# Attention with two score banks: the banks made one tile for joined converts on VectorE, GpSimd instructions in halves, a freer limit for zero-weight passes

## Chip, cores, metric

One core of one Trainium2 chip. The metric is the device time of one execution in microseconds, the median of repeated runs. PE is TensorE, DVE VectorE, ACT ScalarE, POOL GpSimd.

## What must be computed

Two attention blocks over the same input of 2048 rows and 512 columns (32 heads of 16), mixed by a gate per row:

```python
def reference(A_x, A_wqkv, A_wo, B_x, B_wqkv, B_wo, gate_w):
    x = A_x
    g = sigmoid((x * gate_w).sum(-1, keepdims=True))
    a = full_attention(x, A_wqkv, A_wo)          # softmax(q k^T / 4) v, 32 heads, S = 2048
    b = local_dilated_attention(x, B_wqkv, B_wo) # each row sees 8 rows, 2 apart
    return g * a + (1 - g) * b
```

Block A is the bulk: 32 heads x 2048 x 2048 scores, each of which needs an exponential.

## The kernel before

A planner, written in Python, runs while the kernel is built. It places every instruction on its engine by a table of durations and emits them in that order; on the chip each engine follows its fixed order, and semaphores make it wait where data is not there yet. (In the trace of before the 1012 instructions of VectorE, 669 of ScalarE and 589 of GpSimd all start in the order of the built program, compared by what they write and read, and so do 10810 of TensorE's 10822 matmuls; the other 12 have changed places, in pairs, with the one beside them. ScalarE waits 27.5 us for the rings there, in 36 waits.) So the plan's durations never bind the chip (half a multiplication of GpSimd, planned at 600 ns, takes 669 in halves_alone), but its **order** does.

Scores go two ways. Most tiles (128 x 512) are filled by TensorE into one of two "rings" of PSUM banks, and ScalarE takes their exponential. The rest, in quads of four tiles, are filled into one of two single banks, and VectorE "converts" them: one multiply-add with a 16-bit integer result, whose bits read as bfloat16 approximate the exponential, then two additions of a constant for a better fit. The two banks also take every projection of the kernel. GpSimd does the elementwise work of block B. Zero-weight matmul passes ("zero passes") are there to keep TensorE at its full clock: without them the time at half clock (a granted clock of 0.5) grows.

```python
# before: each bank is a buffer of its own (tag m0 or m1), taken anew for each use
def misc_ps(hold, shape, dtype=FP32):
    return ps.tile(shape, dtype, tag=f"m{hold.k}", bufs=1, name=f"m{hold.k}_ps")
# ... one tile of a quad (cut)
def fill(j=j, hold=hold, st=st):
    st["s"] = misc_ps(hold, [128, QW])
    for _ in range(f_.zeros):
        mm_ct(st["s"], zw, ones_t[:], True, True)
    mm(st["s"][:], kt_all[32*j:32*j+32, i, t*128:(t+1)*128], qt_tiles[...], True, True, tile_position=(32*j, 0))
def conv(j=j, st=st):
    V.tensor_scalar(out=q["terms"][0][:, j, :], in0=st["s"][:], scalar1=EXP_MULT, scalar2=EXP_ADD, ...)
# ... GpSimd, block B (cut)
G.tensor_tensor(out=st["prod"][:, w_ % 2, :], in0=st["ksh"][:, w_, :], in1=st["qb"][:], op=ALU.mult)   # planned at 1149 ns
# ... limit for a zero pass (cut)
if sh >= high or after > (first + 60.0 if sh >= low else alone + 230.0):
    return
```

## Time and profile before

| | before |
|---|---|
| time | 806.65 us (3 runs, 806.61 to 809.28) |
| busy | ScalarE 93%, TensorE 91%, VectorE 80%, GpSimd 70% |
| half clock of TensorE, first to last exponential | 41 us in 6 stretches |
| ScalarE idle, first to last exponential | 28 us |
| chain of waits | ScalarE 50%, TensorE 27%, VectorE 11% |

TensorE's share is no measure of its load, as its matmuls overlap: the 1620 fills of the rings, 388 ns each or 629 us one after another, keep it busy for 277.8 us. ScalarE's share is a better one, as its instructions overlap by only 0.2 us each. The last row follows the execution back from its end, at each step to what released the instruction: half of the span is exponentials that followed one another. This is its line on the page of before ("issue" is time for which the profile shows no cause; SPq, ACTq and DVEq are the instruction queues of SyncE, ScalarE and VectorE):

```profile
ACT 50%; PE 27%; DVE 11%; issue 9%; SPq 2%; DMA 1%; ACTq 0%; DVEq 0%
```

Engines, clock and waits of before are shown in the prediction below.

### The profile page before, as it was taken

The numbers are of one execution on the slowest core, as the hardware profiler recorded it, in microseconds if no ns is written. First come the engines' busy times: TensorE is split into PE (matmuls) and PEld (weight loads), VectorE is DVE, ScalarE is ACT, GpSimd is POOL, SyncE is SP. The second block draws the span as 40 slices with busy tenths as digits, with TensorE's granted clock in tenths as the row PEclk, the third lists the DMA queues.
The fourth block names the chain that finished last, engine by engine and source line by source line (L and its number), as shares of the span: only waits on it lengthen the run. The fifth ranks groups of instructions, "written<-read, shape, count | busy, mean of one in ns | idle before, by whom it ended". The sixth has DMA issues, their size and how long they took to land.

```text
span 806.9 us, 24993 instructions
## 1 busy us (share of the span) xinstructions
PE 736.5 (91%) x10822; PEld 245.6 (30%) x10822; DVE 649.1 (80%) x1012; ACT 747.0 (93%) x670; POOL 561.1 (70%) x589
## 2 busy tenths in 40 slices
PE   7898999998898999999989999988999899999996
PEld 3242232323232223333233223323233223322332
DVE  5757997788977767889978999997879997777765
ACT  2998898999999979999999999999899999999991
POOL 1017888598519957697969698979788898995500
PEclk9999998999999879999999999999899999999998
DMA  9332031422302221414211404031313130402000
GB/s 205 106 112 86 30 104 48 139 87 72 105 3 98 81 77 49 140 35 138 81 47 35 137 5 132 19 102 58 108 53 112 34 105 25 142 24 84 9 15 34
DMA packets 66798, 62.07 MB, mean 77 GB/s; under 512 B 14848, under 2 KB 64128, under 8 KB 66688
## 3 DMA queue, kind: packets, MB, share of 16 engines
q1 hardware_dynamic: 65104, 60.28, 24.0%
q8 instruction: 84, 1.38, 0.7%
q10 hardware_dynamic: 1584, 0.20, 0.2%
q14 instruction: 26, 0.21, 0.1%
HBM read 43.91 MB, written 12.62 MB: 70 GB/s over the span
## 4 chain that ended last, share of the span: by engine, by line
ACT 50%; PE 27%; DVE 11%; issue 9%; SPq 2%; DMA 1%; ACTq 0%; DVEq 0%
ACT pT L390 49%; PE m_ps L390 11%; PE acc L390 9%; DVE dt L390 8%; PE ring L390 7%; SPq L390 2%; DVE qr L390 1%; ACT lg L390 1%; DMA xT<-in_A_x_dram 0%; DVE accT L390 0%; DVE kvs L390 0%; DVE osb L390 0%; DVE kmax_all L390 0%; DVE vd_all L390 0%; DMA kt_all<-kr 0%
## 5 line engine op out<-in xcount | busy, mean ns | idle before, releaser
L390 ACT ACTIVATE pT<-ring 128x1536 bf16<-128x1536 f32 (+1 forms) x648 | 741.9, 1335 | 28.7 <-PE ring L390 27.5
L390 DVE TENSOR_SCALAR dt<-m_ps 128x512 uint16<-128x512 f32 x428 | 283.7, 680 | 74.1 <-PE m_ps L390 57.2
L390 PE MATMUL ring<-qt,kt_all 32*128 32x512 bf16 x1620 | 277.8, 388 | 39.7 <-ACT pT L390 34.9
L390 DVE TENSOR_SCALAR dt<-dt 128x2048 uint16<-128x2048 uint16 x214 | 203.6, 964 | 3.0 <-PE acc L390 1.9
L390 PEld LDWEIGHTS <-kt_all 32*128 32x128 bf16 (+1 forms) x2304 | 95.0, 91 | 312.9 <-issue 299.5
L390 POOL TENSOR_TENSOR prod<-prod 128x512 f32<-128x512 f32 (+2 forms) x192 | 175.4, 914 | 8.8
L390 POOL TENSOR_TENSOR prod<-ksh,qb 128x512 f32<-128x512 bf16 x128 | 158.5, 1257 | 11.4 <-DMA ksh<-kv_scr 8.8
L390 POOL TENSOR_TENSOR pv<-vsh,lg 128x512 bf16<-128x512 bf16 x128 | 152.5, 1198 | 15.4 <-PE m_ps L390 13.9
L390 PE MATMUL m_ps<-qt,kt_all 32*128 32x512 bf16 x428 | 148.7, 386 | 10.4 <-DVE dt L390 7.3
L390 PE MATMUL acc<-pT,vp_all 128*17 128x512 bf16 x1620 | 133.4, 390 | 0.0
L390 POOL TENSOR_TENSOR ott<-accT,rden 128x256 bf16<-128x256 f32 x31 | 24.1, 777 | 89.6 <-DVE rden L390 89.5
L390 PE MATMUL acc<-dt,vd_all 128*17 128x512 bf16 x856 | 76.3, 385 | 0.0
L390 PE MATMUL acc<-ones_t,zw 128*32 128x512 bf16 x744 | 66.4, 393 | 0.0
L390 PE MATMUL m_ps<-bw,xT 128*32 128x512 bf16 x768 | 59.4, 406 | 3.6 <-DVE kvs L390 2.0
L390 PEld LDWEIGHTS <-vp_all 128*17 128x17 bf16 x2048 | 41.9, 89 | 68.4 <-issue 55.1
L390 PEld LDWEIGHTS <-xT 128*32 128x32 bf16 (+1 forms) x1920 | 34.5, 98 | 36.9 <-issue 28.6
L390 PE MATMUL acc<-dt,vp_all 128*17 128x512 bf16 x428 | 42.5, 388 | 0.0
L390 POOL TENSOR_TENSOR lg<-lg,mx 128x256 f32<-128x256 f32 x16 | 12.0, 748 | 41.8 <-DVE mx L390 41.8
L390 PE MATMUL m_ps<-ident,pv 128*32 128x128 bf16 x2048 | 39.3, 220 | 0.2 <-DVE dt L390 0.2
L390 POOL TENSOR_TENSOR lg<-lg,rr 128x256 f32<-128x256 f32 x16 | 10.7, 670 | 40.2 <-DVE rr L390 34.2
L390 DVE CAST kvs<-m_ps 128x512 bf16<-128x512 f32 x32 | 21.8, 683 | 17.4 <-PE m_ps L390 17.1
L390 PEld LDWEIGHTS <-pv 128*32 128x32 bf16 x2048 | 30.4, 96 | 14.8 <-issue 11.8
(82 smaller groups left out, 412.8 us busy)
## 6 DMA issues: line engine op xcount, KB each, us to landing
ksh<-kv_scr SPq DMA_DIRECT2D x16, 1024.0 KB
vsh<-kv_scr SPq DMA_DIRECT2D x16, 1024.0 KB
kv_scr<-kvs SPq DMA_DIRECT2D x16, 384.0 KB
q_scr<-qr SPq DMA_DIRECT2D x32, 128.0 KB
qt<-q_scr SPq DMA_DIRECT2D x31, 128.0 KB
qb<-kv_scr SPq DMA_DIRECT2D x16, 128.0 KB
out_dram<-osb SPq DMA_DIRECT2D x16, 128.0 KB
kt_all<-kr SPq DMA_DIRECT2D x112, 16.0 KB
```

The lines of the kernel that those rows point to most:

```text
L390: return chain_on(key, f(*a, **k))
```

## The change

Its intent: relieve VectorE by converting two tiles in one instruction where both banks are free; let VectorE's additions be held up less by GpSimd, by halving GpSimd's long instructions; and admit more zero passes where the activity that the planner counts is low. How GpSimd holds them up is seen in the trace of before: 141 of the 214 additions of 128x2048 see a GpSimd instruction end while they run, and they themselves end 545 to 683 ns after it, 550 at the median. To convert two banks in one instruction, the change makes them one tile: `mm_t` replaces the two buffers. (The diff is shortened; `...` marks a cut. A count that goes with the halves, from 25 to 37 instructions of GpSimd, is left out.)

```diff
-    def misc_ps(hold, shape, dtype=FP32):
-        return ps.tile(shape, dtype, tag=f"m{hold.k}", bufs=1, name=f"m{hold.k}_ps")
+    mm_t = ps.tile([128, 2, QW], FP32, tag="mm", bufs=1, name="mm_ps")
+    def misc_ps(hold, shape):
+        v = mm_t[:, hold.k, 0:math.prod(shape[1:])]
+        ...
-            if sh >= high or after > (first + 60.0 if sh >= low else alone + 230.0):
+            if sh >= high or after > (first + 60.0 if sh >= low else alone + 450.0):
-            padd(lmul(w_), 1149.0, ...)                    # and amul 1094, ltree 1260
+            padd(lmul(w_, 0), 600.0, ...)                  # two halves; amul 575, ltree 630
+        def conv(j):
+            V.tensor_scalar(out=q["terms"][0][:, j:j + 2, :] if j in both else q["terms"][0][:, j, :],
+                            in0=mm_t[:] if j in both else mm_t[:, holds[j].k, :], ...)
+        def join(j, at):     # called when fill j (0 or 2) is placed
+            if S_.slots["m"].when(2) + (MARGIN["DVE", "PE"] if at > 25000.0 else 0.0) > at + JOIN:   # JOIN = 100
+                return
+            both.add(j)      # one fill of two matmuls, one convert of 1217 ns
```

More of the change, by code (lines that the diff above doesn't have):

```diff
@@ L78 @@
                  "name", "not_before", "after", "begun", "prompt", "zeros", "closing",
-                 "lock", "gap", "kb")
+                 "lock", "gap", "kb", "ahead")
     def __init__(self, eng, fn, dur=0.0, mms=None, deps=(), due=None, allow=1000.0, acq=(), rel=(), lat=0.0,
@@ L83, in __init__ @@
                  lock=False, kb=0.0):
+        self.ahead = None
         self.kb = kb
@@ L207, in commit @@
         e = op.eng
+        if op.ahead is not None:
+            op.ahead(max(ready, self.t[e]))
         for h in op.acq:
@@ L418 @@
         S_.slots["keep"].free[k] = INF
-    def misc_ps(hold, shape, dtype=FP32):
-        return ps.tile(shape, dtype, tag=f"m{hold.k}", bufs=1, name=f"m{hold.k}_ps")
+    mm_t = ps.tile([128, 2, QW], FP32, tag="mm", bufs=1, name="mm_ps")
+    def misc_ps(hold, shape):
+        v = mm_t[:, hold.k, 0:math.prod(shape[1:])]
+        if len(shape) > 2:
+            v = v.rearrange("p (a b) -> p a b", a=shape[1])
+        return v
     def sb(hold, shape, dtype, name):
@@ L897, in padd @@
         def padd(fn, dur, after_last=True, early=False, **kw):
-            late = len(pool) > 25 and not early
+            late = len(pool) > 37 and not early
             o = Op("POOL", fn, dur=dur, due=float(2 * t + (3 if late else 0)), name="bp", **kw)
@@ L903, in padd, with lmul @@
             return o
-        def lmul(w_):
+        HD = D // 2
+        def lmul(w_, lo):
             def s():
-                if w_ % 2 == 0:
+                if w_ % 2 == 0 and lo == 0:
                     st["prod"] = work.tile([128, 2, D], FP32, name="prod", tag="prod", bufs=1)
@@ L910, in s, with ltree @@
                         st["lg"] = sb(hlg, [128, H, W], FP32, "lg")
-                G.tensor_tensor(out=st["prod"][:, w_ % 2, :], in0=st["ksh"][:, w_, :], in1=st["qb"][:], op=ALU.mult)
+                G.tensor_tensor(out=st["prod"][:, w_ % 2, lo:lo + HD], in0=st["ksh"][:, w_, lo:lo + HD], in1=st["qb"][:, lo:lo + HD],
+                                op=ALU.mult)
             return s
-        def ltree(w_, n):
+        def ltree(w_, n, a=0, b=2):
             def s():
-                pv_ = st["prod"][:].rearrange("p w (h d) -> p w h d", d=DH)
+                pv_ = st["prod"][:, a:b, :].rearrange("p w (h d) -> p w h d", d=DH)
                 if n > 1:
@@ L923, in b_tile @@
         for w_ in range(0, W, 2):
-            padd(lmul(w_), 1149.0, after_last=w_ > 0, acq=[hlg] if w_ == 0 else [], deps=[lk] if w_ == 0 else [])
-            padd(lmul(w_ + 1), 1149.0, after_last=False)
-            padd(ltree(w_, 8), 1260.0)
+            padd(lmul(w_, 0), 600.0, after_last=False, acq=[hlg] if w_ == 0 else [], deps=[lk] if w_ == 0 else [])
+            for w2, lo in ((w_, HD), (w_ + 1, 0), (w_ + 1, HD)):
+                padd(lmul(w2, lo), 600.0, after_last=False)
+            padd(ltree(w_, 8, 0, 1), 630.0, after_last=False)
+            padd(ltree(w_, 8, 1, 2), 630.0, after_last=False)
             padd(ltree(w_, 4), 630.0)
@@ L971, in b_tile, with amul @@
         obt_hold[t] = Hold("keep")
-        def amul(w_):
+        def amul(w_, g):
             def s():
-                if w_ == 0:
+                if w_ == 0 and g == 0:
                     st["pv"] = work.tile([128, W, D], BF16, name="pv", tag="pv", bufs=1)
-                a0 = st["lg"][:, :, w_:w_ + 1]
-                attn_bc = _ap(a0, [list(a0.ap[0]), [W, H], [0, DH]])
-                G.tensor_tensor(out=st["pv"][:, w_, :].rearrange("p (h d) -> p h d", d=DH),
-                                in0=st["vsh"][:, w_, :].rearrange("p (h d) -> p h d", d=DH), in1=attn_bc, op=ALU.mult)
+                a0 = st["lg"][:, g * H // 2:(g + 1) * H // 2, w_:w_ + 1]
+                attn_bc = _ap(a0, [list(a0.ap[0]), [W, H // 2], [0, DH]])
+                G.tensor_tensor(out=st["pv"][:, w_, g * HD:(g + 1) * HD].rearrange("p (h d) -> p h d", d=DH),
+                                in0=st["vsh"][:, w_, g * HD:(g + 1) * HD].rearrange("p (h d) -> p h d", d=DH), in1=attn_bc, op=ALU.mult)
             return s
         for w_ in range(W):
-            padd(amul(w_), 1094.0, after_last=w_ == 0, acq=[hpv] if w_ == 0 else [], deps=[lv] if w_ == 0 else [],
-                 rel=[hvs, hlg] if w_ == W - 1 else [])
+            padd(amul(w_, 0), 575.0, after_last=w_ == 0, acq=[hpv] if w_ == 0 else [], deps=[lv] if w_ == 0 else [])
+            padd(amul(w_, 1), 575.0, after_last=False, rel=[hvs, hlg] if w_ == W - 1 else [])
         def wsum(c):
@@ L1386 @@
     quad_end = [None]
+    JOIN = 100.0
     def soon(o, late):
@@ L1432, in make_quad @@
         aops, fops = [], []
-        for j in range(4):
-            hold = Hold("m")
-            st = {}
-            def fill(j=j, hold=hold, st=st):
-                f_ = fops[j]
-                st["s"] = misc_ps(hold, [128, QW])
-                for _ in range(f_.zeros):
-                    mm_ct(st["s"], zw, ones_t[:], True, True)
-                mm(st["s"][:], kt_all[32 * j:32 * j + 32, i, t * 128:(t + 1) * 128],
-                   qt_tiles[periods[p]][32 * j:32 * j + 32, :], True, True, tile_position=(32 * j, 0))
-            def conv(j=j, st=st):
-                if j == 0:
-                    term_tile()
-                V.tensor_scalar(out=q["terms"][0][:, j, :], in0=st["s"][:], scalar1=EXP_MULT, scalar2=EXP_ADD,
-                                op0=ALU.mult, op1=ALU.add)
-            f_ = S_.add(Op("PE", fill, mms=[("r", j, 512)], deps=[qt_ops[periods[p]][0], kdep(p, t)],
+        holds, both = [Hold("m") for _ in range(4)], set()
@@ new lines, in fill @@
+        def fill(j):
+            f_ = fops[j]
+            for _ in range(f_.zeros):
+                mm_ct(mm_t[:, 0 if j in both else holds[j].k, :], zw, ones_t[:], True, True)
+            for j_ in ((j, j + 1) if j in both else (j,)):
+                mm(mm_t[:, j_ - j if j in both else holds[j].k, :], kt_all[32 * j_:32 * j_ + 32, i, t * 128:(t + 1) * 128],
+                   qt_tiles[periods[p]][32 * j_:32 * j_ + 32, :], True, True, tile_position=(32 * j_, 0))
+        def conv(j):
+            if j == 0:
+                term_tile()
+            V.tensor_scalar(out=q["terms"][0][:, j:j + 2, :] if j in both else q["terms"][0][:, j, :],
+                            in0=mm_t[:] if j in both else mm_t[:, holds[j].k, :], scalar1=EXP_MULT, scalar2=EXP_ADD,
+                            op0=ALU.mult, op1=ALU.add)
@@ new lines, in join, with same @@
+        def join(j, at):
+            f1, f2, a1, a2 = fops[j], fops[j + 1], aops[j], aops[j + 1]
+            if S_.slots["m"].when(2) + (MARGIN["DVE", "PE"] if at > 25000.0 else 0.0) > at + JOIN:
+                return
+            both.add(j)
+            S_.pend["PE"].remove(f2)
+            S_.pend["DVE"].remove(a2)
+            f1.mms = f1.mms + f2.mms
+            f1.acq += f2.acq
+            a1.rel += a2.rel
+            a1.dur = 1217.0
+            def same(o, o2):
+                o2.start, o2.fin, o2.vis = o.start, o.fin, o.vis
+            f1.after = lambda o: same(o, f2)
+            a1.after = lambda o: same(o, a2)
@@ L1451, in make_quad @@
+        for j in range(4):
+            f_ = S_.add(Op("PE", lambda j=j: fill(j), mms=[("r", j, 512)], deps=[qt_ops[periods[p]][0], kdep(p, t)],
                            begun=fops[-1:] or [quad_end[0]], allow=0.0,
-                           acq=[hold] + ([] if j else hq[:1]), name="fillD"))
+                           acq=[holds[j]] + ([] if j else hq[:1]), name="fillD"))
             fops.append(f_)
             quad_end[0] = f_
-            a_ = S_.add(Op("DVE", conv, dur=683.0, deps=[f_] + aops[-1:], due=min(S_.now, late - 6000.0) + 300.0 * j - 5000.0, rel=[hold],
-                           name="conv"))
+            a_ = S_.add(Op("DVE", lambda j=j: conv(j), dur=683.0, deps=[f_] + aops[-1:], due=min(S_.now, late - 6000.0) + 300.0 * j - 5000.0,
+                           rel=[holds[j]], name="conv"))
@@ L1457, in make_quad @@
             aops.append(a_)
+            if j % 2 == 0:
+                f_.ahead = lambda at, j=j: join(j, at)
         tops = []
```

## The prediction

> **What bounds the kernel now.** I read the page's table of engines first, then the clock row, then the groups of instructions by shape, then the table of waits.
>
> ```profile
> span 806.9 us, 24993 instructions
> ...
> PE 736.5 (91%) x10822; PEld 245.6 (30%) x10822; DVE 649.1 (80%) x1012; ACT 747.0 (93%) x670; POOL 561.1 (70%) x589
> ...
> PEclk9999998999999879999999999999899999999998
> ...
> L390 ACT ACTIVATE pT<-ring 128x1536 bf16<-128x1536 f32 x324 | 501.6, 1548 | 13.4 <-PE ring L390 12.8
> L390 ACT ACTIVATE pT<-ring 128x1024 bf16<-128x1024 f32 x324 | 363.7, 1122 | 15.4 <-PE ring L390 14.7 <-PE m_ps L390 0.4
> ```
>
> ScalarE is busy 747.0 of 806.9 us: the exponentials bound the kernel. Its 60 us of idle, by stretches of the span: 15.7 before 20 us, 2.1 to 60 us, 19.6 to 400, 5.0 to 700, 1.3 to 790, and 16.4 in the tail after its last exponential. What can be won in the middle is therefore some 28 us and no more, plus whatever work leaves ScalarE. Six stretches at half clock (42.0 us together, granted clock 0.50 to 0.59) hold 12.6 us of that idle.
>
> ```profile
> POOL ott L390 <- DVE rden L390: 89.5, 16, 47.5
> DVE dt L390 <- PE m_ps L390: 57.2, 87, 2.1
> ...
> PE ring L390 <- ACT pT L390: 38.2, 101, 0.9
> ...
> ACT pT L390 <- PE ring L390: 27.5, 36, 2.7
> ...
> PE m_ps L390 <- DVE dt L390: 10.8, 24, 1.2
> ```
>
> Today TensorE hardly waits for VectorE at the two score banks (10.8 us in 24 waits), and ScalarE waits for TensorE only 27.5 us. A piece of the timeline shows why (start, duration):
>
> ```profile
> 505.41 0.69 DVE L390 TENSOR_SCALAR dt<-m_ps 128x512 uint16<-128x512 f32 x1 [0.34 <-PE m_ps L390]
> ...
> 505.85 0.39 PE L390 MATMUL m_ps<-qt,kt_all 32*128 32x512 bf16 x1
> ...
> 506.27 0.69 DVE L390 TENSOR_SCALAR dt<-m_ps 128x512 uint16<-128x512 f32 x1 [0.17 <-PE m_ps L390]
> ```
>
> The fill of one bank starts at 505.85 while VectorE still converts the other bank, until 506.10. That overlap is what the two banks are for.
>
> [...]the trace has a median of 681 for 512[...]the 128x2048 additions take 622 ns at least, 742 at the median, 964 on average and 2357 at most. [...]the six stretches here last 3.5 to 17.1 us at about 0.5[...].
>
> **The change, part by part**, from counting both built programs.
>
> Exponentials: 1620 score tiles on ScalarE become 1608, because 110 instead of 107 quads of tiles go to VectorE. ScalarE loses two 1536-wide and three 1024-wide instructions. The 648 instructions overlap by (501.6 + 363.7 - 741.9) / 648 = 0.19 us each, so the saving is 2 x (1.548 - 0.190) + 3 x (1.122 - 0.190) = 5.5 us, all of it on the bounding engine.
>
> Joined converts: only 21 of the possible 220 pairs are joined (398 single converts remain). [...]The three added quads cost VectorE 3 x (4 x 0.68 + 2 x 0.74) = 12.6 us.
>
> GpSimd in halves: 128 + 128 multiplications and 64 additions are split, 320 more instructions. 512 columns take 1157 ns at the median and 256 take 628 to 632, so a split costs about 0.1 us less some overlap: 20 to 30 us more on an engine that is 70% busy, harmless. In return a 128x2048 addition waits behind shorter instructions: it loses 214 x (964 - 622) = 73 us[...] at most; I take a third back, some 25 us of VectorE, again off the path.
>
> Zero passes: the loads of zero weights fall from 788 to 772, so there are not more passes, only better placed ones. They could win part of the 12.6 us; stalls of TensorE (next) would lose it again. I count zero.
>
> The two banks become **one tile**. This is the part that the diff's wording hides. Before, each bank was its own buffer; after, both are views of one tile with an access pattern of 1024 columns per partition. I followed each semaphore wait in the built programs to the instruction that satisfies it. Before, 544 matmuls into these banks wait for VectorE, each for the last reader of its own bank. After, 396 do, and 315 of them wait for a reader of the **other** bank, one that comes later. One instance: a fill of bank 1 waits for VectorE's count 406, the convert of bank 0, while the last read of bank 1 was count 404. In the same way converts wait for the other bank's fill. So the overlap shown at 505.85 is forbidden: a fill must now wait until the other bank has been converted.
>
> What that costs, from the trace of before: I paired its records with its program in order and asked what the new rule would have meant. Of 440 fills that would have to wait for the other bank, 353 began while that read was running, with 0.66 us to go on average (50 ns for the semaphore included). Sorted by what precedes a fill, the 315 waits after fall into 150 where the other bank was filled before both reads (0.32 us on average in the trace), 82 where own read, other fill and other read follow each other (0.54), 45 with both banks filled and only the other read (1.09), 24 where own fill and then other fill come before the other read (0.55) and 14 rest: 48 + 44 + 49 + 13 + 10 = 164 us of stalls on TensorE, if nothing gives way. TensorE runs in order, so the next fill of the exponentials' ring is late too. From the end of a ring fill to its exponential the trace has 0.27 us at the median and never less than about 0.10, so the real slack is 0.17 us: applied to each stall in turn, two thirds reaches ScalarE, some 110 us. Much of that gives way: VectorE has 158 us of idle and TensorE 70, and where ScalarE is late, later reads have ended before their fills come. I choose 40% of it, 44 us; this is the softest number here.
>
> Sum: 806.65 - 5.5 + 44 = about 845 us.
>
> **The rivals.** (1) The waits are harmless: in the changed order the reads have nearly always ended. Then 5.5 us leave ScalarE, and better zero passes bring up to 8 more: 793 to 801. For it speaks that a kernel tuned this finely is not usually changed for a worse one; against it the 80% of fills that would have met a running read. I give it a quarter. (2) VectorE becomes the bound: reads with no other VectorE instruction between them and the read that released their fill rise from 25 to 142 in the programs. Each exposes semaphore, fill (0.39) and semaphore, about 0.5 us: 117 x 0.5 = 59 us more idle within VectorE's chain. 649 + 12.6 - 3 - 25 + 59 = 693 us still fits, but it leaves little room for catching up: 860 to 890. (3) The stalls thin out TensorE's activity, half-clock stretches multiply, and each takes about 2 us from ScalarE as the six do now: 10 to 20 us on top.
>
> **Range and chances.** Between 845 from the mechanism and about 798 from the first rival, weighted three to one, I predict 834 us, with 794 to 885 as the range. Slower by over 2% is above 822.8: it needs only 22 us of net loss from stalls worth up to 110, so 0.66. Within 2%: 0.26. Faster by over 2% (below 790.5) would need the waits to be harmless and nearly all half-clock stretches gone: 0.08.
>
> **What would show it.** Right: TensorE's waits at the two banks for VectorE rise from 10.8 us to over 60; ScalarE's idle before exponentials, put down to the ring, from 27.5 to over 60; ScalarE's busy time falls to about 741; VectorE waits longer for fills than 57 us; the additions fall from 964 to about 850 ns[...]. No fill starts while a convert of the other bank runs. Wrong: those waits stay under 20 us and ScalarE's idle is unchanged; then the first rival holds. If waits are large but the span is not, the stalls were hidden, and my two thirds failed.

In rival 2's sum of 693 us the "- 3" comes from the 21 joined converts; these take 1213 ns on average in the changed kernel, where two single ones of before take 2 x 681 (the median), so by these measured figures it is 21 x 0.15 = 3.1 us. Five of the statements need numbers beside them:

- **A 128x2048 addition waits behind GpSimd's instructions**: it ends 550 ns (median) after the one that ends while it runs, as said above.
- **TensorE runs in order**: 10810 of its 10822 matmuls start in the program's order, as said above.
- **The semaphore's 50 ns**: in the trace of before, a fill that waits for a convert starts 53 ns after the convert's end (median of 24 waits), and a convert that waits for a fill 38 ns after the fill's (87 waits).
- **Zero passes help the clock, and stalls of TensorE bring half clock** (zero passes, rival 3): runs made later show both. Half clock is 41 us in before and 229 without these passes; it is 205 us in the changed kernel and 31 with its banks apart (after_two_tiles).
- **"Never less than about 0.10" from a ring fill's end to its exponential**: a recount in the trace of before gives the same median, 0.27 us, but 49 of the 648 lie under 0.10, the least at 0.04. The slack of 0.17 us was an estimate of mine.

## The result

The changed kernel takes **966.4 us** (4 runs, 963.09 to 969.73) against 807.01 us: 1.197 times as long, with a 95% interval of 1.191 to 1.203. The outputs are correct. The direction was forecast; the size was not: 966 lies far outside 794 to 885.

The page of the changed kernel: engines, clock, and the chain that ended last.

```profile
span 961.9 us, 25343 instructions
...
PE 800.3 (83%) x10830; PEld 252.0 (26%) x10830; DVE 640.0 (67%) x1009; ACT 765.5 (80%) x665; POOL 608.3 (63%) x909
...
PEclk9988899997987999899779989999967599779797
...
PE 54%; DVE 32%; ACT 8%; issue 4%; DMA 0%; DVEq 0%; ACTq 0%
```

No engine is busy for more than 83% of the span, and ScalarE has left the chain: 50% before, 8% now. The kernel is now bound by TensorE and VectorE in turns. When no engine is full and the chain alternates between two, look for a loop of waits between those two. The table of waits names it (engine, what waited, for whom; total, times, longest):

```profile
DVE dt L393 <- PE mm_ps L393: 135.3, 144, 4.0
ACT pT L393 <- PE ring L393: 132.5, 186, 4.1
PE mm_ps L393 <- DVE dt L393: 94.1, 164, 1.6
```

TensorE's waits for VectorE's converts at the two banks rose from 10.8 us to 94.1, and with its waits for VectorE's other reads of the banks from 18.9 us (34 waits) to 136.1 us (221). ScalarE's waits for the ring rose from 27.5 to 132.5 us. One turn of the loop, from the timeline of the changed kernel (start, duration, engine, instruction, idle before it and what ended that):

```profile
602.94 0.69 DVE L393 TENSOR_SCALAR dt<-mm_ps 128x512 uint16<-128x512 f32 x1 [2.18 <-PE mm_ps L393]
...
603.55 0.68 DVE L393 CAST bw<-mm_ps 128x512 bf16<-128x512 f32 x1
...
604.28 0.37 PE L393 MATMUL mm_ps<-qt,kt_all 32*128 32x512 bf16 x1 [1.18 <-DVE bw L393]
...
604.29 0.39 PE L393 MATMUL ring<-qt,kt_all 32*128 32x512 bf16 x3
...
604.69 0.69 DVE L393 TENSOR_SCALAR dt<-mm_ps 128x512 uint16<-128x512 f32 x1 [0.46 <-PE ring L393]
604.77 1.45 ACT L393 ACTIVATE pT<-ring 128x1536 bf16<-128x1536 f32 x1 [0.62 <-PE ring L393]
```

Matching these records with the program tells the banks. The convert at 602.94 reads bank 1 and ends at 603.63; the cast at 603.55 reads bank 0 and ends at 604.23. The fill at 604.28 writes **bank 1**, free for 0.65 us by then, and yet TensorE stood idle for 1.18 us until the read of bank 0 was over. The ring's fill comes behind it in order, and ScalarE idles for 0.62 us. Counted over the whole trace in the same way, 185 of the 565 first writes to a bank after a read of it begin while the other bank is being read in before; after the change it is 0 of 577.

Where the 155.0 us between the two profiled spans are, all on ScalarE: it starts 4.3 us later; its idle between first and last exponential grows by 64.0 us at full clock (15.5 to 79.5) and by 62.6 us at half clock (12.5 to 75.1, as half clock grows from 41 to 205 us); it is busy 18.4 us longer there, although 12 tiles have left it; and the tail is 5.6 us longer. The busy time has its explanation in these two groups, to be read beside the ones of before in the prediction (busy time, mean of one, idle before):

```profile
L393 ACT ACTIVATE pT<-ring 128x1536 bf16<-128x1536 f32 x322 | 470.7, 1462 | 80.5 <-PE ring L393 73.4 <-PE mm_ps L393 3.9
L393 ACT ACTIVATE pT<-ring 128x1024 bf16<-128x1024 f32 x321 | 332.6, 1036 | 74.2 <-PE ring L393 59.2 <-PE mm_ps L393 13.4
```

The mean of one is shorter than before, and the sum of busy time is longer: exponentials that follow one another at once overlap (0.19 us each before, by the prediction's sum), and after an idle gap nothing overlaps. By the same sum the overlap is now (470.7 + 332.6 - 758.1) / 643 = 0.07 us (758.1 is their joint busy time). Looked at one by one, 61 exponentials of before start after a gap and 274 of the changed kernel. Those of before that start after a gap take about 0.1 us less at either width (1456 against 1558 ns, 1045 against 1130), and the others overlap the one before them by 0.21 us. So, as an estimate from these figures, a gap costs its own length and about 0.1 us more; 213 more gaps make some 23 us, and the 5.5 us of the tiles that left come off it.

### The profile page after: what moved, and what is told of

The parts are those of the page before. It is cut to its first block, busy times and chain, and to the rows that moved or that the text cites. A ratio compares the mean times of both kernels' runs of the same rounds, so it can differ in the third digit from the quotient of the medians.

```text
span 961.9 us, 25343 instructions
## 1 busy us (share of the span) xinstructions
PE 800.3 (83%) x10830; PEld 252.0 (26%) x10830; DVE 640.0 (67%) x1009; ACT 765.5 (80%) x665; POOL 608.3 (63%) x909
## 4 chain that ended last, share of the span: by engine, by line
PE 54%; DVE 32%; ACT 8%; issue 4%; DMA 0%; DVEq 0%; ACTq 0%
PE mm_ps L393 29%; DVE dt L393 22%; PE acc L393 15%; PE ring L393 9%; ACT pT L393 8%; DVE kvs L393 2%; DVE qr L393 1%; DVE kr L393 1%; DVE kt_all L393 1%; DVE vp_all L393 1%; DVE osb L393 1%; DVE accT L393 1%; DVE kmax_all L393 1%; PE warm L393 1%; DVE bw L393 1%
## 5 line engine op out<-in xcount | busy, mean ns | idle before, releaser
L393 ACT ACTIVATE pT<-ring 128x1536 bf16<-128x1536 f32 (+1 forms) x643 | 758.1, 1249 | 154.7 <-PE ring L393 132.5
L393 DVE TENSOR_SCALAR dt<-mm_ps 128x512 uint16<-128x512 f32 (+1 forms) x419 | 292.7, 710 | 178.4 <-PE mm_ps L393 135.3
L393 PE MATMUL ring<-qt,kt_all 32*128 32x512 bf16 x1608 | 306.6, 419 | 11.9 <-ACT pT L393 9.8
L393 PE MATMUL mm_ps<-qt,kt_all 32*128 32x512 bf16 x440 | 159.3, 424 | 78.7 <-DVE dt L393 57.7
L393 POOL TENSOR_TENSOR pv<-vsh,lg 128x256 bf16<-128x256 bf16 x256 | 175.0, 706 | 32.6 <-PE mm_ps L393 17.7
L393 POOL TENSOR_TENSOR prod<-ksh,qb 128x256 f32<-128x256 bf16 x256 | 180.9, 736 | 16.4 <-DMA ksh<-kv_scr 12.6
L393 POOL TENSOR_TENSOR prod<-prod 128x256 f32<-128x256 f32 (+1 forms) x256 | 183.6, 727 | 5.6
L393 PE MATMUL mm_ps<-bw,xT 128*32 128x512 bf16 x768 | 61.8, 416 | 17.2 <-DVE dt L393 11.7
L393 POOL TENSOR_TENSOR lg<-lg,rr 128x256 f32<-128x256 f32 x16 | 10.7, 669 | 75.7 <-DVE rr L393 67.7
L393 PE MATMUL mm_ps<-ident,pv 128*32 128x128 bf16 x2048 | 40.7, 222 | 6.4 <-DVE dt L393 5.6
L393 DVE CAST kvs<-mm_ps 128x512 bf16<-128x512 f32 x32 | 21.7, 683 | 25.8 <-PE mm_ps L393 21.9
L393 PEld LDWEIGHTS <-zw 128*32 128x32 bf16 x772 | 19.2, 102 | 70.6 <-issue 67.0
```

Of the source, the lines that this page charges most:

```text
L393: return chain_on(key, f(*a, **k))
```

## The experiments

Theory 1: the shared tile is nearly the whole loss, since it makes fills and reads of the two banks wait for each other. Its rivals: the halves, the joins or the freer limit. Theory 2, beside it: much of the loss is the lower clock that the stalls bring. And then the question why my estimate of the size fell so short.

| run | what differs | median us | ratio to before (95%) | half clock us |
|---|---|---|---|---|
| changed kernel | | 966.4 | 1.197 (1.191 to 1.203) | 205 |
| one_tile_alone | before + shared tile | 960.98 | 1.185 (1.179 to 1.191) | 202 |
| after_no_join | changed, no joins | 961.39 | 1.185 (1.179 to 1.191) | 188 |
| after_two_tiles | changed, two tiles | 816.51 | 1.007 (1.001 to 1.013) | 31 |
| halves_and_limit | changed, two tiles, no joins | 822.46 | 1.014 (1.005 to 1.023) | 65 |
| halves_alone | before + halves | 819.51 | 1.013 (1.008 to 1.017) | 65 |
| limit_alone | before + limit 450 | 811.67 | 1.003 (0.998 to 1.007) | 41 |
| no_zero_passes | before, no filler passes | 848.54 | 1.048 (1.043 to 1.054) | 229 |
| changed_kept_warm | changed, more zero passes | 931.07 | 1.149 (1.142 to 1.156) | 45 |
| one_tile_planned | one_tile_alone, plan knows | 864.49 | 1.068 (1.063 to 1.073) | 52 |
| one_bank_planned | before, one bank | 1005.35 | 1.245 (1.239 to 1.252) | 54 |
| halves_timed | halves_alone, true durations | 802.27 | 0.994 (0.989 to 0.999) | 34 |
| halves_timed_limit | the same + limit 450 | 804.62 | 0.991 (0.985 to 0.997) | 34 |
| changed_planned | changed, plan knows, true durations | 856.77 | 1.061 (1.057 to 1.066) | 32 |
| changed_planned_nojoin | the same, no joins | 863.01 | 1.065 (1.060 to 1.071) | 27 |

Half clock is between the first and the last exponential of the profiled run. All outputs were correct. The medians are of all runs, the ratios of fast ones only (one run of changed_kept_warm and one of halves_timed_limit were slow). The kernel before ran beside each set and took 802 to 815 us in its fast runs, a wider spread than at first, so differences under 1% rest on the intervals alone.

### The shared tile by itself

```diff
 # one_tile_alone: on the kernel before, nothing else
-        return ps.tile(shape, dtype, tag=f"m{hold.k}", bufs=1, name=f"m{hold.k}_ps")
+        v = mm_t[:, hold.k, 0:math.prod(shape[1:])]   # mm_t one tile [128, 2, 512]; rest cut
```

> The kernel before with one edit: the two score banks become two views of one tile; the order of instructions on every engine stays that of before, no joins, no halves, old limit for zero passes. Theory 1 (the shared tile makes fills and reads of the two banks wait for each other, and that is nearly the whole loss): 930 to 970 us, TensorE's waits for VectorE at the two banks over 100 us, ScalarE's idle before exponentials over 100 us. Rival (the loss is in the halves, the joins or the freer zero passes): 806 to 815 us.

The order of instructions on every engine is that of before, instruction for instruction. Measured: 960.98 us. Its waits:

```profile
ACT pT L390 <- PE ring L390: 141.8, 190, 2.5
DVE dt L390 <- PE mm_ps L390: 133.4, 159, 4.3
PE mm_ps L390 <- DVE dt L390: 94.3, 165, 1.5
```

They are those of the changed kernel within a few per cent. The one edit is enough for the loss.

```diff
 # after_two_tiles: the changed kernel, order as planned there
+            for j_ in js:
+                st[j_] = misc_ps(holds[j_], [128, QW])      # a buffer per bank again
-            V.tensor_scalar(out=...[:, j:j + 2, :], in0=mm_t[:], ...)
+            for j_ in (j, j + 1) if j in both else (j,):     # a joined convert becomes two
+                V.tensor_scalar(out=...[:, j_, :], in0=st[j_][:], ...)
```

> The changed kernel with one edit: the two banks are two tiles again; the planned order on every engine stays that of the changed kernel, and each of the 21 joined converts becomes two single ones. Theory 1: back to 795 to 812 us, since 5.5 us of exponentials have left ScalarE. Rival (halves, joins or zero passes cost the time): stays above 900 us.

Measured: 816.51 us. With the shared tile taken out and the plan unchanged, the changed kernel is 0.7% slower than before instead of 19.7%. TensorE's waits are back, too:

```profile
ACT pT L393 <- PE ring L393: 24.8, 35, 2.8
PE m_ps L393 <- DVE dt L393: 13.5, 31, 1.5
```

So the shared tile is necessary and sufficient for nearly the whole loss. My expected range ended at 812, and the 5.5 us that left ScalarE (it is busy 742.3 us here, against 747.0) did not shorten the span: something in the rest of the change costs about 10 us.

```diff
 # after_no_join: shared tile kept      # halves_and_limit: two tiles as above, and
-    JOIN = 100.0
+    JOIN = -INF
```

> The changed kernel with the shared tile but no joins. Theory 1: the joins are no part of the loss, so 940 to 980 us, within 2% of the changed kernel. Rival (waiting for two fills before one long convert is what stalls): under 900 us.

> The changed kernel with two tiles and no joins at all: GpSimd in halves and freer zero passes alone (the same instructions as these two edits on the kernel before). The plan now gives ScalarE 1600 tiles instead of 1620, some 9 us less. Theory 1: 790 to 806 us. If halves or the freer limit hurt by themselves: above 815 us.

Measured: 961.39 and 822.46 us. The joins are not what stalls. And halves with the freer limit, without any of the bank business, are slower than before, against my expectation.

### Halves and limit apart

```diff
 # halves_alone: on the kernel before, the three GpSimd edits of the change
 # limit_alone:  on the kernel before
-            ... else alone + 230.0):
+            ... else alone + 450.0):
```

> The kernel before with GpSimd's multiplications and first additions in halves, nothing else (1616 tiles on ScalarE instead of 1620, some 2 us less). The run with halves, limit and two tiles came out 1.4% slower than before. If the halves cause that: 812 to 824 us here, with the 128x2048 additions on VectorE above 964 ns on average[...]. If the limit causes it: 802 to 809 us, additions about 850 ns as I first predicted.

> The kernel before with the freer limit for zero passes alone (828 loads of zero weights instead of 788, 1612 tiles on ScalarE). If better placed passes keep the clock up: half-clock time under 41 us between first and last exponential, 800 to 807 us. If more passes only push the fills of the ring back: 809 to 820 us.

Measured: 819.51 and 811.67 us. The limit by itself changes nothing that these runs resolve, and half clock stays at 41 us. The halves cost 1.3%. But not by longer additions, as I had offered: VectorE's 128x2048 additions take 914 ns on average, less than the 964 of before, and only 2 of 216 take over 1.5 us, against 34 of 214. That GpSimd is what lengthens them is borne out by before: the 55 additions beside which no GpSimd instruction runs take 697 ns at most, the other 159 take 1062 on average and up to 2357, and the 141 that see a GpSimd instruction end do so 550 ns after it (median). The halving does what it was meant to do. The additions in before and in halves_alone (busy time, mean of one, idle before):

```profile
L390 DVE TENSOR_SCALAR dt<-dt 128x2048 uint16<-128x2048 uint16 x214 | 203.6, 964 | 3.0 <-PE acc L390 1.9
```

```profile
L390 DVE TENSOR_SCALAR dt<-dt 128x2048 uint16<-128x2048 uint16 x216 | 194.6, 914 | 5.4 <-PE acc L390 3.9
```

What the halving does besides, from the waits of halves_alone:

```profile
ACT lg L390 <- POOL lg L390: 12.8, 9, 2.4
DVE mx L390 <- POOL lg L390: 7.5, 6, 2.3
```

Neither line is among the waits of before. ScalarE, which bounds the kernel, waits in its order for GpSimd's subtraction in block B. (Half clock also rises, from 41 to 65 us. But of the 14.0 us that ScalarE's idle grows by between its exponentials, 10.7 lie at full clock and 3.3 at half clock, so it is the smaller part.) And GpSimd is late because its halves are not half as long. The lines of before and of halves_alone (minimum, median, maximum in ns; then first and last start):

```profile
L390 POOL TENSOR_TENSOR prod<-ksh,qb x128: 1146/1157/1617, 61.9 to 733.0; 128x512 f32<-128x512 bf16 x128
```

```profile
L390 POOL TENSOR_TENSOR prod<-ksh,qb x256: 658/669/1199, 63.3 to 736.5; 128x256 f32<-128x256 bf16 x128
```

Two halves take 1338 ns where one whole took 1157, and the plan had put a half at 600. By the spacing of the starts of consecutive ones it is 2 x 628 against 1114 ns. A straight line through the spans leaves 181 ns for an instruction of no length, one through the spacings 142: an estimate from these four figures.

```diff
 # halves_timed: on halves_alone, durations in the plan only; halves_timed_limit: and alone + 450.0
-            padd(lmul(w2, lo), 600.0, ...)      # amul 575.0, ltree 630.0
+            padd(lmul(w2, lo), 669.0, ...)      # amul 639.0, ltree 720.0
```

> halves_alone (1.3% slower than before) with the plan's durations of the halved GpSimd instructions set to what the traces show: 669 instead of 600 ns for half a multiplication, 639 instead of 575 for half a weighting, 720 instead of 630 for half an addition. If the halves hurt because the plan takes GpSimd to be faster than it is and everything that waits for GpSimd comes late: 800 to 811 us, no slower than before. If they hurt by themselves: 815 to 825 us.

> The same with the freer limit for zero passes: the version that would carry two of the three edits without their costs. 1608 tiles on ScalarE, 5.5 us less than before. 796 to 812 us; a version better than before only if under 803.

Measured: 802.27 and 804.62 us, ratios 0.994 and 0.991 with intervals that end below 1. Not one instruction of GpSimd got faster; the plan only knows what they take. ScalarE's and VectorE's waits for GpSimd shown above are gone from the list of halves_timed, and half clock is down to 34 us. So the halves hurt by a wrong number in the plan, and with the right one these versions come out 0.6 and 0.9% faster than before: the best here. Two things keep that gain from being the halves' alone. The new plan leaves 1608 tiles on ScalarE instead of 1620, which by the prediction's sum is some 5.5 us, about the whole of it. And the 720 also corrects an addition that was never halved: the plan of before has it at 630, and it takes 728 there. Before with that one number put right was not run, so what the halves are worth by themselves is not shown. The limit of 803 us that I had set for halves_timed_limit was missed by its median (803.03 without its one slow run, which is not in the ratio).

### What the clock costs

```diff
 # no_zero_passes: on the kernel before       # changed_kept_warm: on the changed kernel
-    S_.filler = zero_pass                     -STREAM = 0.48
+    S_.filler = None                          +STREAM = 0.62   (and LEAST 0.42 -> 0.56)
```

> The kernel before without any filler passes, to price the low clock by itself, banks separate. The changed kernel has 205 us of half clock between first and last exponential and ScalarE idles in 37% of it, against 11% of the rest: by that the clock is worth some 50 of its 155 us. Theory 2 (much of the loss is the lower clock that the stalls bring): here 200 to 400 us of half clock, and 0.25 us of time per us of half clock, so 850 to 900 us. Rival (the clock is a side effect that costs next to nothing): within 2% of 807 us whatever the clock.

> The changed kernel, shared tile and all, with both thresholds of activity raised by 0.14 so that its plan lets in 1760 loads of zero weights instead of 772. Theory 2: half clock falls below 80 us and the time by 30 to 60 us, to 905 to 940 us. Rival (the waits themselves are all): clock back to over 0.96, time unchanged or longer than 966 us, as the passes also take TensorE's time.

Measured: 848.54 us with 188 us more half clock, and 931.07 us with 160 us less. By the ratios, that is 0.048 x 809 = 39 us gained by 188 us of half clock, and (1.197 - 1.149) x 809 = 39 us won back by 160 us less: both give 0.21 to 0.24 us per us of half clock. The two plans also differ otherwise from the kernels that they are compared with (8 tiles fewer on ScalarE in the first, 12 more and 39 joins in the second); at 0.46 us a tile, an estimate, the prices would be 0.23 and 0.28. So about a quarter of the changed kernel's loss is the lower clock, and it comes from the stalls: with two tiles half clock is 31 us. With the clock nearly whole, 120 us of loss remain, so theory 2 is right as a part and wrong as the cause.

### Why the stalls cost so much

```diff
 # one_tile_planned: one_tile_alone, and the planner is told
+            if h.res == "m":      # a fill comes after every read of either bank already placed
+                w = max([w] + [f for f in self.slots["m"].free if f < INF])
+        if op.eng != "PE" and any(h.res == "m" for h in op.rel):
+            e = max(e, self.m_filled)      # a read comes after the last fill placed
```

> The kernel before with the shared tile (as in one_tile_alone, 961 us), but the planner knows: a fill is planned after every read of the two banks already placed, a read after the last fill placed. The waits in the program remain (219 of its fills wait for the other bank's reader); the plan leaves ScalarE 1652 tiles instead of 1620, some 15 us more. Theory A (TensorE is in order, and the loss is so large because the plan puts the ring's fills behind fills that it believes free): 840 to 890 us. Rival B (the waits themselves cost it, however planned): 930 us or more.

> The kernel before with a single score bank instead of two, planned as such: 1696 tiles left on ScalarE, some 35 us more. If the shared tile in effect makes one bank of two: within 4% of one_tile_planned. If the second bank keeps a good part of its worth in pairs of fills and reads: over 4% longer than one_tile_planned.

Measured: 864.49 us. Counted as the 315 of the changed kernel were, 269 of its matmuls still wait for the other bank's reader (321 in one_tile_alone; the 219 of the expectation is too low), and no first write begins during a read of the other bank; only the plan was made with these waits in mind. That takes back (1.185 - 1.068) x 809 = 95 us of 150. Of the waits, TensorE's fall to a quarter, and ScalarE's to a third; VectorE's stay:

```profile
DVE dt L397 <- PE mm_ps L397: 134.4, 129, 3.0
...
ACT pT L397 <- PE ring L397: 49.2, 57, 7.1
...
PE mm_ps L397 <- DVE dt L397: 24.6, 44, 1.7
```

and ScalarE leads the chain again:

```profile
ACT 40%; PE 32%; DVE 17%; issue 10%; DMA 1%; ACTq 0%; DVEq 0%; SPq 0%
```

So most of the loss was not the serialized banks but a plan that takes them to be free: the ring's fills stand behind a fill that cannot start. VectorE waits as long as in one_tile_alone (134 us), and that is affordable; TensorE's waits are not. The clock's part is within the 95 us: half clock falls from 202 to 52 us, and this plan also places more zero passes (1112 loads of zero weights instead of 788). What the order is worth at a like clock can be estimated from two other rows: changed_kept_warm has 45 us of half clock, changed_planned (below) 32, both made from the changed kernel, and between them lie (1.149 - 1.061) x 809 = 71 us. These two also differ in the planned durations of GpSimd (some 15 us, by halves_alone and halves_timed) and, the other way, in 32 tiles more on ScalarE (some 15 us). Of the 55 us that remain, some 15 are the 32 tiles that this plan leaves on ScalarE (32 x 0.46 us).

one_bank_planned (`("m", 2)` becomes `("m", 1)`) takes 1005.35 us. I had set "within 4% of one_tile_planned" as the mark of a shared tile that makes one bank of two: it is 16% or 141 us longer, and its 44 tiles more on ScalarE are only some 20 of these. Two banks that wait for each other still allow a pair of fills and then a pair of reads: in the trace of the changed kernel the first writes to the two banks follow one another 184 times with no read begun between them.

### The joins

```diff
 # changed_planned: the changed kernel + the planner edit above + durations of halves_timed
 # changed_planned_nojoin: the same with JOIN = -INF
```

> The changed kernel with a plan that knows the shared tile's waits, and with the measured durations of the halved GpSimd instructions. 85 pairs of converts are joined. One joined convert takes 1.21 us against 2 x 0.68: 85 x 0.15 = 13 us of VectorE. If the joins pay: 840 to 858 us, 1% or more under the version without joins. If not: within 1% of it.

> The same without joins: 850 to 868 us, like one_tile_planned (864 us).

Measured: 856.77 us with 85 pairs joined, 863.01 us with none; ratios 1.061 and 1.065, whose intervals overlap. By my own mark (within 1%) the joins are not shown to pay. A joined read of two banks that are separate tiles was not tried, so what joins would bring without the shared tile stays open; at 0.15 us each and VectorE off the path I estimate that it would be little.

## Why the prediction was wrong

The mechanism was right, and so was the sign; the step that failed is the discount for what gives way, which left the term for what reaches ScalarE two to three times too small.

- **ScalarE relieved by 5.5 us**: right. Its busy time fell by 4.7 us where the banks were separate (after_two_tiles).
- **Joined converts**: 1213 ns on average, 0.15 us less than two single ones, 3.1 us in all, and no gain in time (966.4 us with joins, 961.39 without).
- **Fills wait for the other bank's reader**: right, and shown. Of first writes during the other bank's read 185 became 0. The prediction's "353 began while that read was running" was loosely put: it also counted reads that came earlier in the program and had not begun on the chip.
- **164 us of stalls on TensorE**: about right; 136 us in 221 waits were measured.
- **"Much of that gives way ... I choose 40% of it, 44 us"**: this step failed. TensorE's waits for VectorE at the banks grew by 117 us, and ScalarE's idle between its exponentials by 126.6 us (28.0 to 154.6), not 44. Some 39 us of that go with the half clock (rival 3 below). The 88 us that remain are, as an estimate, 75% of what the stalls grew by: near the two thirds before the discount, and twice the 44 after it. So little gave way, and the loss as a whole was about 155 us. I reasoned that VectorE's 158 us and TensorE's 70 us of idle would take up the lateness. They could not here, where two engines wait for each other in fixed orders: a late fill makes a late convert, and that makes the next fill late. The idle of an average is not slack in a loop. The waits grew on both sides (VectorE's converts for fills by 78 us, TensorE for reads by 117), and ScalarE's gaps followed. I took each stall by itself and asked how much reaches ScalarE; the right question was how long one turn of the loop takes. That lateness runs round the loop is read from the chain of waits; what the runs prove is that 95 us of the 150 hang on the plan, better clock included, and, as an estimate, some 70 on the order at a like clock.
- **Overlap of exponentials**: left out of the sum; with gaps between them ScalarE's busy time grew by 18 us instead of falling by 5.
- **Rival 2, VectorE becomes the bound, 860 to 890 us**: the nearest of the estimates. Its 59 us more of exposed waits were 78 for the converts. But VectorE is busy for only 67% of the span, and one_tile_planned keeps 134 us of these waits and takes 864 us; so VectorE's waits by themselves are not what makes 966.
- **Rival 3, half clock, 10 to 20 us**: the mechanism was right (205 us of half clock against 41, and 31 with two tiles), the size 39 us.
- **Halves cost nothing, a third of 73 us back on VectorE**: wrong in both. A split costs 0.14 to 0.18 us per multiplication, not 0.1, GpSimd's busy time rose by 64 us (561.1 to 624.9 in after_two_tiles) and not by 20 to 30, and what waits for it came late, 1.3% in halves_alone. The additions became 0.05 us shorter each there, 11 us. That the additions of the changed kernel do take 859 ns, close to the 850 forecast, is partly luck: one_tile_alone, without halves, has 904 against 964.
- **Zero passes count zero**: right, 1.003 in limit_alone.
- **First rival, harmless waits, a quarter**: given for the reason that a tuned kernel is not changed for a worse one. That is no evidence about a mechanism, and it pulled the central value from 845 to 834.

## What to carry to other kernels

Making two buffers views of one tile can put a wait between them that no line of the source shows (here 315 matmuls wait for a read of the other bank); before trusting double buffering, look in the built program for whom each wait names. In a statically ordered kernel, a stall on an engine that feeds the bound can be paid nearly in full when the order puts the feeding instructions behind it, however much idle time the averages show (here 117 us more of stalls, and 127 us more of idle on ScalarE, some 39 of them with the half clock); teach the plan the wait, or take it away. And a duration in a plan must be measured for the new size, not halved: here 70 ns too few per instruction made the difference between 0.6% faster and 1.3% slower than before.
